# A decode kernel's second MLP weight: 18 rows on each of 96 partitions in place of 13 on 128 and 64 rows apart

## The chip, the core and the metric

The kernel runs on one core of a Trainium2 chip. The core has five engines with instruction streams of their own: TensorE (PE; its weight loads are listed as PEld), VectorE (DVE), ScalarE (ACT), GpSimd (POOL) and SyncE (SP), which here only issues transfers. They meet by semaphores. Sixteen transfer (DMA) engines move data between the chip's main memory and the on-chip memory of 128 partitions; SP and ACT each have a queue that feeds all sixteen. The metric is the device time of one execution in microseconds, lower being better. Before the change it is 1282.53 us, the median of three runs (1282.53 to 1282.58).

## The reference, cut to what matters

One step of decoding for eight sequences. Two branches work on the same normalized input and are added to it: attention over a cache of 4096 keys with 32 heads, and an MLP.

```python
def _A_ref(x, k_cache, v_cache, wq, wo):          # x: 8 x 1 x 640
    q = (x @ wq).reshape(B, Sq, 32, 128).transpose(0, 2, 1, 3)
    scores = einsum("bhqd,bhkd->bhqk", q, k_cache) * (128 ** -0.5)   # k_cache: 8 x 32 x 4096 x 128
    o = einsum("bhqk,bhkd->bhqd", softmax(scores), v_cache)
    return o.transpose(0, 2, 1, 3).reshape(B, Sq, 32 * 128) @ wo

def _B_ref(x, w1, b1, w2, b2):                    # w1: 640 x 1728, w2: 1728 x 640
    h = gelu(layernorm(x) @ w1 + b1)
    return h @ w2 + b2

xn = layernorm(x)
return x + _A_ref(xn, ...) + _B_ref(xn, ...)
```

All inputs are bf16. The two caches are 537 MB together; everything else is under 15 MB.

## The kernel before

The attention is cut into 32 steps (NQ): each takes one sequence and eight heads, so that a tile of K or V holds 256 keys on each of 128 partitions (16 partitions to a head), 64 KB to a partition, 8.4 MB in all. There are three such slots in the on-chip memory (`S_sb`): two for K in turn (KA, KB) and one for V. In each step VectorE multiplies 176 of the 256 keys with the query and adds up; TensorE transposes the other 80 and multiplies them; ScalarE takes the exponentials; TensorE sums V with 256 small matmuls.

The order of work is written by hand. Every piece is put at a position by `at(position, function)` (lines 775 to 863), step i having positions from 100 i on, and the pieces are then run in order of position; each appends its instructions to the stream of its engine and takes the tickets (semaphore values) of what it needs. PE, DVE and ACT replay their streams as hardware loops; that of PE (`_replay_pe`, line 163) has 32 turns, and what belongs to the last steps alone, the MLP with it, stands inside the loop behind branches that skip it in all other turns.

SP issues nearly all transfers, in one queue: A_wq, then K and V of each step. A load of K waits until the K of two steps before has been used by TensorE and VectorE (`load_k`, line 356), a load of V until the V before has been used (`load_v`, line 369). `load_mlp` (line 364) waits for the K of step 30 to be used, whose slot then takes the MLP's weights, and issues w1 and the larger part of w2. V of step 31 is issued next, and then, once the last K has been used, five pieces of A_wo (`load_wl`, `load_wn`).

ACT issues the few small loads: x, b2 and the last 64 rows of w2 (w2b) at the start, b1 near the end, and the store of the result.

The MLP's weights lie as follows. w1 (640 x 1728) has five rows on each of 128 partitions. F = 1728 = 13 x 128 + 64: w2's first 1664 rows are laid 13 to a partition, so partition p has rows 13p to 13p + 12, one run of 16,640 bytes; the last 64 rows have a small tile of their own, one row to a partition. `pe_mlp1` (line 494) works out the hidden layer in 14 chunks: chunk c < 13 takes w1's columns c, c + 13, c + 26, ... (128 of them), so that its results stand on the partitions where w2's rows for them are; the fourteenth takes the last 64 columns. Each chunk is five matmuls over the input and one for the bias, into a region of a bank of the accumulator memory (`HT_ps`, 8 columns to a chunk). `act_gelu` (line 505) applies the gelu in two instructions, one to 128 partitions and 13 chunks, one to 64 partitions and the last. `pe_mlp2` (line 512) multiplies with w2, five matmuls to a chunk, and adds to the bank that holds the final sum.

On TensorE the MLP stands in the last turn between V's matmuls of step 30 and those of step 31 and among the selections (`pe_selw`, `pe_sel`), which bring the attention's outputs into the layout of A_wo and whose results VectorE folds (`dve_foldw`, `dve_fold`). After V's matmuls of step 31 come the products with A_wo (`fin_wl`, `fin_wn`), a transpose and the store.

Of the kernel before, what the change touches and what calls it, by code (L numbers as in the profile page):

```python
# [8 lines left out]
BF = mybir.dt.bfloat16  # L9
F32 = mybir.dt.float32  # L10
I32 = mybir.dt.int32
ACT = mybir.ActivationFunctionType
AX = mybir.AxisListType

P = 128
# [177 lines left out]
def bass_parallel_sum__gqa_block_cached__mixer_channel_mlp__decode_kernel(  # L193
# [13 lines left out]
    B, _, D = A_x.shape  # L207
    _, H, SK, DH = A_k_cache.shape
    F = B_w1.shape[1]
# [4 lines left out]
    NHQ = H // HS  # L214
    NQ = NHQ * B
    DC = D // P
    FB = F // P
    FLAST = F - FB * P
    SCALE = float(DH) ** -0.5
    TPB = 8  # L220
    NS = 2
# [3 lines left out]
    KA, KB, VS = 0, 1, 2  # L225
# [24 lines left out]
    with ExitStack() as es:  # L250
        sb = lambda name, shape, dt: es.enter_context(nc.sbuf_tensor(name, shape, dt))
        ps = lambda name, shape, dt: es.enter_context(nc.psum_tensor(name, shape, dt))
        sem = lambda name: es.enter_context(nc.semaphore(name))
# [4 lines left out]
        def part(slot, lo, n, rows=P):  # L258
            return S_sb[0:rows, slot, lo:lo + n]
# [3 lines left out]
        def scratch(n, rows=P, slot=KB):  # L263
            ap = part(slot, o_[slot], n, rows)
            o_[slot] += n + n % 2
            return ap

        wq_sb = part(VS, 0, DC * H * DH).rearrange("p (c n) -> p c n", c=DC)
        w1_sb = scratch(DC * F, P, KA).rearrange("p (c n) -> p c n", c=DC)
        w2_sb = scratch(FB * D, P, KA).rearrange("p (c n) -> p c n", n=D)  # L270
        hT_sb = scratch((FB + 1) * B, P, KA).rearrange("p (c b) -> p c b", b=B)
        b1_sb = scratch(F, 1, KA)
        selW_sb = scratch(HW * P, P, KA).rearrange("p (c h r) -> p c h r", c=HW, h=HW)
        sel_sb = scratch(HS * P, P, KA).rearrange("p (c h r) -> p c h r", c=HS, h=HS)
# [13 lines left out]
        assert max(o_.values()) <= SLOT  # L288

        ones_sb = sb("ones_sb", [1, B], BF)  # L290
        w2b_sb = sb("w2b_sb", [FLAST, D], BF)
        xT_sb = sb("xT_sb", [P, 2, DC, B], BF)
        KT_sb = sb("KT_sb", [P, NS, TPB, P], BF)
        Sd_sb = sb("Sd_sb", [P, 2, NKEY], F32)
# [26 lines left out]
        TR_ps = ps("TR_ps", [P, 2, TPB * P], BF)  # L321
# [4 lines left out]
        ACC_ps = ps("ACC_ps", [P, 512], F32)  # L326
        TRB, SBK = [_Bank(), _Bank()], [_Bank(), _Bank()]
        PVB, QBB, CHB, ACCB = _Bank(), _Bank(), _Bank(), _Bank()
        QT_ps = CH_ps[:, 0:H * B]
        HT_ps = TR_ps[:, 1, :].bitcast(F32)[:, 0:(FB + 1) * B]  # L330
        RS_ps = CH_ps[:, 384:384 + HS]
        OUT_ps = QB_ps[:, :].bitcast(BF)
        assert H * B <= 384
# [1 line left out]
        pe, dve, act, sp, pool = (_Eng(sem(f"{n}_s")) for n in ("pe", "dve", "act", "sp", "pool"))  # L335
        pe2, act2 = _Eng(sem("pe2_s")), _Eng(sem("act2_s"))
        ld_s = [_Dma(sem(f"ld_s{s}")) for s in range(3)]
        ld_x, ld_b1, ld_b2, ld_wq, ld_w1, ld_w2a, ld_w2b, st_o = (
            _Dma(sem(n)) for n in ("ld_x", "ld_b1", "ld_b2", "ld_wq", "ld_w1", "ld_w2a", "ld_w2b", "st_o"))
        ld_vl = [_Dma(sem(f"ld_vl{q}")) for q in range(1, len(V_CUT) - 1)]  # L340
        ld_wl = [_Dma(sem(f"ld_wl{q}")) for q in range(2)]
        ld_wn = [_Dma(sem(f"ld_wn{q}")) for q in range(len(WN_CUT) - 1)]
        tk = {}
        prog = []

        def at(pos, fn, *a):
            prog.append((pos, len(prog), fn, a))

        def load(key, dma, dst, src, eng=None):
            tk[key] = dma.sig((eng or sp).dma_start(dst, src))  # L350
# [13 lines left out]
        def load_mlp():  # L364
            sp.wait(tk[("kt", NQ - 2)], tk[("km", NQ - 2)])
            load("w1", ld_w1, w1_sb, B_w1.rearrange("(p c) f -> p c f", c=DC))
            load("w2a", ld_w2a, w2_sb, B_w2[0:FB * P, :].rearrange("(p c) n -> p c n", c=FB))

        def load_v(i):
            sp.wait(tk["qmm"] if i == 0 else tk[("pv", i - 1)])  # L370
# [117 lines left out]
                pe.matmul(ACC_ps[:, c * B:(c + 1) * B], b2_sb[:, c * P:(c + 1) * P], ones_sb[:, :],  # L488
                          start=False, stop=False, skip_group_check=True)

        def fcols(c):
            return (slice(c, FB * P, FB), P) if c < FB else (slice(FB * P, F), FLAST)

        def pe_mlp1():
            pe.wait(tk["w1"], tk["b1"], tk[("xT", 1)])
            TRB[1].use(pe)
            for c in range(FB + 1):
                cols, rows = fcols(c)
                o = HT_ps[0:rows, c * B:(c + 1) * B]
                for kc in range(DC):  # L500
                    pe.matmul(o, w1_sb[:, kc, cols], xT_sb[:, 1, kc, :], start=(kc == 0), stop=False)
                last = pe.matmul(o, b1_sb[:, cols], ones_sb[:, :], start=False, stop=True)
            TRB[1].used(pe, pe.sig(last))

        def act_gelu():
            TRB[1].use(act)
            act.activation(hT_sb[:, 0:FB, :].rearrange("p c b -> p (c b)"), HT_ps[:, 0:FB * B],
                           ACT.Gelu_apprx_tanh)
            tk["h"] = TRB[1].used(act, act.sig(act.activation(
                hT_sb[0:FLAST, FB, :], HT_ps[0:FLAST, FB * B:(FB + 1) * B], ACT.Gelu_apprx_tanh)))  # L510

        def pe_mlp2():
            pe.wait(tk["h"], tk["w2a"], tk["w2b"])
            for fc in range(FB + 1):
                rows = P if fc < FB else FLAST
                w = w2_sb[:, fc, :] if fc < FB else w2b_sb
                for c in range(DC):
                    last = pe.matmul(ACC_ps[:, c * B:(c + 1) * B], w[:, c * P:(c + 1) * P],
                                     hT_sb[0:rows, fc, :], start=False, stop=False, skip_group_check=True)
            tk["mlp"] = ACCB.used(pe, pe.sig(last))  # L520


# [254 lines left out]
        at(-898, load, "b2", ld_b2, b2_sb, B_b2.rearrange("(o f) -> o f", o=1), act)  # L777
        at(-890, load, "wq", ld_wq, wq_sb, A_wq.rearrange("(p c) n -> p c n", c=DC))
        at(NQ * Q - 55, load_mlp)
        at(-897, load, "w2b", ld_w2b, w2b_sb[:, :], B_w2[FB * P:F, :], act)  # L780
        at(-870, load_k, 0)
        at(-800, consts_pool)
        at(-795, idents)
# [10 lines left out]
        at(-765, cp_q)  # L794
        at(NQ * Q - 11.8, load_b1)
        at(NQ * Q - 11.5, pe_mlp1)
        at(NQ * Q - 11, act_gelu)
        at(NQ * Q + 4.6, pe_mlp2)
        for i in range(NQ):
            o = i * Q  # L800
            last = i == NQ - 1
# [8 lines left out]
            w = 42.0 / nt  # L810
# [20 lines left out]
        o = NQ * Q  # L831
# [76 lines left out]
```

## Time and profile before

| | |
|---|---|
| median of three runs | 1282.53 us |
| profiled execution | 1282.34 us |
| its span, first to last instruction | 1281.0 us |
| busy: VectorE / TensorE / ScalarE / GpSimd | 1103.0 / 672.2 / 476.1 / 100.0 us |
| moved | 551.99 MB, 431 GB/s over the span |
| TensorE's granted clock, mean | 0.557 |

The span is the time between the first and the last instruction of the execution that was profiled; the rest of its time lies around it. "Busy" is the time in which an engine has at least one instruction under way. The profile has further views: forty equal slices of the span with the busy tenths of each engine and of the transfer engines; the transfers by queue and by issue, with the time from issue to landing; the chain that ended last, followed back from the end; the timeline, in which each row has its start, its duration, engine, line, operation, and in brackets how long the engine had been idle and what ended that; and tables of busy time and GB/s by windows. In them q1 is SP's queue, q10 is ACT's, and q8 and q14 fetch instructions. Nearly all instructions carry line 111, that of the helper which emits them, so they are told apart by the tiles that they write and read; w1, w2 and A_wo lie in `S_sb`, as K and V do. The trace also has a record of every packet: one row of a transfer, moved by one of the sixteen engines, with its queue, start, duration and bytes.

### The profile page before, as it was taken

How to read it: one execution, taken by the hardware profiler on the slowest of the kernel's cores; microseconds unless marked ns; L12 is line 12 of the kernel's file. 1: busy time of each engine (PE TensorE's matmuls, PEld its weight loads, DVE VectorE, ACT ScalarE, POOL GpSimd, SP SyncE). 2: the span in 40 equal slices, each digit the busy share in tenths (PEclk: the TensorE clock that was granted, in tenths of full speed). 3: DMA queues.
4: the chain of work that ended last, by engine and by line, in shares of the span. 5: the costliest groups of instructions: out<-in, count | busy, mean ns of one | idle time of the engine just before them, and what ended most of it. 6: DMA issues, size and time to landing. Idle time of an engine off the chain costs nothing.

```text
span 1281.0 us, 34439 instructions
## 1 busy us (share of the span) xinstructions
PE 672.2 (52%) x13944; PEld 575.5 (45%) x13944; DVE 1103.0 (86%) x680; ACT 476.1 (37%) x905; POOL 100.0 (8%) x110
## 2 busy tenths in 40 slices
PE   1546555446545446555456554456454466464476
PEld 1435445345534345444345444345343355353365
DVE  1899999889888899888898888898888898888895
ACT  0524444233444233443234443234443234442331
POOL 0000010000000000000000000000000000000040
PEclk9755565555555555555565565555555565555565
DMA  9999999999999999999999999999999999999998
GB/s 400 445 422 436 432 432 434 434 436 432 432 432 440 428 432 436 440 426 432 438 438 428 430 436 442 428 430 436 440 430 428 436 436 436 426 438 432 432 439 361
DMA packets 10675, 551.99 MB, mean 431 GB/s; under 512 B 1244, under 2 KB 1445, under 8 KB 1702
## 3 DMA queue, kind: packets, MB, share of 16 engines
q1 hardware_dynamic: 10512, 551.70, 99.7%
q8 instruction: 9, 0.15, 0.0%
q10 hardware_dynamic: 150, 0.11, 0.0%
q14 instruction: 4, 0.03, 0.0%
HBM read 551.80 MB, written 0.01 MB: 431 GB/s over the span
## 4 chain that ended last, share of the span: by engine, by line
DMA 52%; DVE 36%; issue 11%; DVEq 0%; PE 0%; SPq 0%; ACT 0%
DMA S_sb<-in_A_k_cache_dram 51%; DVE S_sb L111 26%; DVE Sd_sb L111 8%; DMA S_sb<-in_A_wo_dram 2%; DVE S_ps L111 1%; DVE ri_sb L111 0%; DVEq L109 0%; PE ACC_ps L111 0%; DVE mx_sb L111 0%; SPq L111 0%; DVE mbT_sb L111 0%; DVE mxT_sb L111 0%; DVE mq_sb L111 0%; DVE mb_sb L111 0%; PE QB_ps L111 0%
## 5 line engine op out<-in xcount | busy, mean ns | idle before, releaser
L111 PE MATMUL TR_ps<-ident_bf,S_sb 128*128 128x128 bf16 (+1 forms) x2570 | 342.9, 280 | 353.5 <-POOL kr_sb L111 341.6
L111 DVE TENSOR_TENSOR S_sb<-S_sb,qbc_sb 128x7552 bf16<-128x7552 bf16 (+1 forms) x96 | 392.6, 4089 | 128.4 <-DMA S_sb<-in_A_k_cache_dram 128.1
L111 PEld LDWEIGHTS TR_ps<-ident_bf,S_sb 128*128 (+2 forms) x2570 | 245.4, 103 | 411.6 <-issue 337.7
L111 DVE TENSOR_REDUCE Sd_sb<-S_sb 128x59 f32<-128x3776 bf16 (+1 forms) x96 | 390.2, 4064 | 6.0
L111 ACT ACTIVATE KT_sb<-TR_ps 128x1024 bf16<-128x1024 bf16 x320 | 326.5, 1023 | 122.0 <-PE TR_ps L111 110.9
L111 PE MATMUL PV_ps<-P_sb,S_sb 128*128 128x8 bf16 x8192 | 224.0, 175 | 137.4 <-DMA S_sb<-in_A_v_cache_dram 134.5
L111 PEld LDWEIGHTS PV_ps<-P_sb,S_sb 128*128 128x128 bf16 x8192 | 221.5, 103 | 140.1 <-DMA S_sb<-in_A_v_cache_dram 137.3
L111 DVE TENSOR_TENSOR S_sb<-S_sb 128x3776 bf16<-128x3776 bf16 (+1 forms) x96 | 204.6, 2131 | 3.3
L111 ACT ACTIVATE P_sb<-Sd_sb,NB_sb 128x256 bf16<-128x256 f32 x256 | 126.3, 494 | 213.4 <-DVE NB_sb L111 213.4
L111 PE MATMUL S_ps<-qrep_sb,KT_sb 128*128 128x8 bf16 x2560 | 121.9, 177 | 51.6 <-ACT KT_sb L111 48.4
L111 ACT ACTIVATE oU_sb<-PV_ps 128x8 f32<-128x8 f32 x31 | 5.5, 177 | 375.6 <-PE PV_ps L111 375.6
L111 PEld LDWEIGHTS S_ps<-qrep_sb,KT_sb 128*128 128x128 bf16 x2560 | 91.8, 103 | 83.0 <-ACT KT_sb L111 42.1
L111 POOL TENSOR_TENSOR oT_sb<-oU_sb,ri_sb 128x8 bf16<-128x8 f32 x31 | 71.8, 2315 | 378.8 <-DVE S_sb L111 303.2
L111 POOL COPY qrep_sb<-qT_sb 128x128 bf16<-128x128 bf16 x32 | 14.5, 453 | 475.3 <-PE S_ps L111 455.2
L111 ACT ACTIVATION_READ_ACCUMULATOR P_sb<-Sd_sb,NB_sb 128x1 f32 x256 | 47.8, 187 | 0.0
L111 DVE TENSOR_TENSOR S_ps<-S_ps,mask_sb 128x320 f32<-128x320 f32 (+1 forms) x65 | 31.6, 486 | 2.6 <-PE S_ps L111 2.6
L111 DVE TENSOR_REDUCE Sd_sb<-S_ps 128x40 f32<-128x320 f32 x64 | 31.5, 491 | 2.2
L111 PE MATMUL QB_ps<-ident_bf,qrep_sb 128*128 128x128 bf16 x32 | 9.1, 284 | 41.2 <-DVE S_sb L111 21.4
L111 ACT ACTIVATE qbc_sb<-QB_ps 128x128 bf16<-128x128 f32 x32 | 8.9, 277 | 58.0 <-PE QB_ps L111 58.0
L111 POOL MEMSET kr_sb<- 128x1 f32 x32 | 3.1, 98 | 294.7 <-DMA S_sb<-in_A_k_cache_dram 294.7
L111 PEld LDWEIGHTS QB_ps<-ident_bf,qrep_sb 128*128 128x128 bf16 x32 | 3.3, 103 | 44.1 <-ACT oU_sb L111 29.5
L111 PE MATMUL CH_ps<-rs_sb,ones_f 128*128 128x8 f32 x64 | 16.5, 330 | 6.6 <-ACT P_sb L111 6.6
(71 smaller groups left out, 147.0 us busy)
## 6 DMA issues: line engine op xcount, KB each, us to landing
S_sb<-in_A_v_cache_dram SPq DMA_DIRECT2D x1, 6144.0 KB, 26.8
S_sb<-in_A_wq_dram SPq DMA_DIRECT2D x1, 5120.0 KB, 16.0
S_sb<-in_A_wo_dram SPq DMA_DIRECT2D x1, 2560.0 KB, 16.5
S_sb<-in_B_w_dram SPq DMA_DIRECT2D x1, 2160.0 KB, 30.3
S_sb<-in_B_w_dram SPq DMA_DIRECT2D x1, 2080.0 KB, 34.8
S_sb<-in_A_v_cache_dram SPq DMA_DIRECT2D x1, 2048.0 KB, 31.3
S_sb<-in_A_wo_dram SPq DMA_DIRECT2D x1, 1280.0 KB, 19.3
S_sb<-in_A_wo_dram SPq DMA_DIRECT2D x1, 800.0 KB, 20.8
```

Source lines behind the costliest of these rows:

```text
L111: inst = getattr(e, name)(*a, **k)
```

## The change

F = 1728 is also 18 x 96. w2 is loaded in one transfer, with 18 rows on each of 96 partitions: partition p has rows 18p to 18p + 17, one run of 23,040 bytes, and partitions 96 to 127 get none of it. The separate tile and its load on ACT's queue are gone. The hidden layer is worked out in 18 chunks of 96 columns (c, c + 18, c + 36, ...), the gelu is one instruction on 96 partitions, and the outer layer has 18 times five matmuls over 96 rows. w1's layout, the positions of the pieces and all other work are as before.

```diff
-    FB = F // P
-    FLAST = F - FB * P
+    FP = 96
+    FB = F // FP
+    assert FB * FP == F
...
-        w2_sb = scratch(FB * D, P, KA).rearrange("p (c n) -> p c n", n=D)
-        hT_sb = scratch((FB + 1) * B, P, KA).rearrange("p (c b) -> p c b", b=B)
+        w2_sb = scratch(FB * D, FP, KA).rearrange("p (c n) -> p c n", n=D)
+        hT_sb = scratch(FB * B, FP, KA).rearrange("p (c b) -> p c b", b=B)
...
-        w2b_sb = sb("w2b_sb", [FLAST, D], BF)
...
-        HT_ps = TR_ps[:, 1, :].bitcast(F32)[:, 0:(FB + 1) * B]
+        HT_ps = TR_ps[:, 1, :].bitcast(F32)[0:FP, 0:FB * B]
...
-            load("w2a", ld_w2a, w2_sb, B_w2[0:FB * P, :].rearrange("(p c) n -> p c n", c=FB))
+            load("w2", ld_w2, w2_sb, B_w2.rearrange("(p c) n -> p c n", c=FB))
...
-        def fcols(c):
-            return (slice(c, FB * P, FB), P) if c < FB else (slice(FB * P, F), FLAST)
-
         def pe_mlp1():
             pe.wait(tk["w1"], tk["b1"], tk[("xT", 1)])
             TRB[1].use(pe)
-            for c in range(FB + 1):
-                cols, rows = fcols(c)
-                o = HT_ps[0:rows, c * B:(c + 1) * B]
+            for c in range(FB):
+                o = HT_ps[:, c * B:(c + 1) * B]
                 for kc in range(DC):
-                    pe.matmul(o, w1_sb[:, kc, cols], xT_sb[:, 1, kc, :], start=(kc == 0), stop=False)
-                last = pe.matmul(o, b1_sb[:, cols], ones_sb[:, :], start=False, stop=True)
+                    pe.matmul(o, w1_sb[:, kc, c:F:FB], xT_sb[:, 1, kc, :], start=(kc == 0), stop=False)
+                last = pe.matmul(o, b1_sb[:, c:F:FB], ones_sb[:, :], start=False, stop=True)
...
-            act.activation(hT_sb[:, 0:FB, :].rearrange("p c b -> p (c b)"), HT_ps[:, 0:FB * B],
-                           ACT.Gelu_apprx_tanh)
             tk["h"] = TRB[1].used(act, act.sig(act.activation(
-                hT_sb[0:FLAST, FB, :], HT_ps[0:FLAST, FB * B:(FB + 1) * B], ACT.Gelu_apprx_tanh)))
+                hT_sb.rearrange("p c b -> p (c b)"), HT_ps, ACT.Gelu_apprx_tanh)))
...
-            pe.wait(tk["h"], tk["w2a"], tk["w2b"])
-            for fc in range(FB + 1):
-                rows = P if fc < FB else FLAST
-                w = w2_sb[:, fc, :] if fc < FB else w2b_sb
+            pe.wait(tk["h"], tk["w2"])
+            for fc in range(FB):
                 for c in range(DC):
-                    last = pe.matmul(ACC_ps[:, c * B:(c + 1) * B], w[:, c * P:(c + 1) * P],
-                                     hT_sb[0:rows, fc, :], start=False, stop=False, skip_group_check=True)
+                    last = pe.matmul(ACC_ps[:, c * B:(c + 1) * B], w2_sb[:, fc, c * P:(c + 1) * P],
+                                     hT_sb[:, fc, :], start=False, stop=False, skip_group_check=True)
...
-        at(-897, load, "w2b", ld_w2b, w2b_sb[:, :], B_w2[FB * P:F, :], act)
```

More of the change, by code (lines that the diff above doesn't have):

```diff
@@ L337, in bass_parallel_sum__gqa_block_cached__mixer_channel_mlp__decode_kernel @@
         ld_s = [_Dma(sem(f"ld_s{s}")) for s in range(3)]
-        ld_x, ld_b1, ld_b2, ld_wq, ld_w1, ld_w2a, ld_w2b, st_o = (
-            _Dma(sem(n)) for n in ("ld_x", "ld_b1", "ld_b2", "ld_wq", "ld_w1", "ld_w2a", "ld_w2b", "st_o"))
+        ld_x, ld_b1, ld_b2, ld_wq, ld_w1, ld_w2, st_o = (
+            _Dma(sem(n)) for n in ("ld_x", "ld_b1", "ld_b2", "ld_wq", "ld_w1", "ld_w2", "st_o"))
         ld_vl = [_Dma(sem(f"ld_vl{q}")) for q in range(1, len(V_CUT) - 1)]
```

## The prediction

> **What bounds the kernel now.** I read the page's slices first, then the table of transfers, the chain that ended last, the last 40 us instruction by instruction, and the traffic by windows.
>
> ```profile
> span 1281.0 us, 34439 instructions
> DMA  9999999999999999999999999999999999999998
> ...
> q1 hardware_dynamic: 10512, 551.70, 99.7%
> q8 instruction: 9, 0.15, 0.0%
> q10 hardware_dynamic: 150, 0.11, 0.0%
> ```
>
> The transfer engines are at nine tenths or more in all slices but the last, and one queue (q1, SP's) has 99.7% of their time. Nothing else needs to be fast; it must only keep that queue filled.
>
> ```profile
> S_sb<-in_B_w_dram SPq DMA_DIRECT2D x1, 2160.0 KB, 30.3
> S_sb<-in_B_w_dram SPq DMA_DIRECT2D x1, 2080.0 KB, 34.8
> ...
> w2b_sb<-in_B_w_dram ACTq DMA_DIRECT2D x1, 80.0 KB, 14.3
> ```
>
> These are w1, w2a and w2b. w2a, issued with w1, lands 4.5 us after it: it stands in line, and 2080 KB at the 434 GB/s of the windows below need 4.9 us. Among the packet records of the trace each of w2a's 128 rows (16,640 B) took 0.62 us, eight in a row on each of 16 engines: 5.0 us. A row of K or V (65,536 B) took 2.42 us; all of these are 27 GB/s to an engine, steady to some ns, and all of them write 128 partitions.
>
> ```profile
> 1205.00 0.81 SPq L111 DMA_DIRECT2D S_sb<-in_A_v_cache_dram  x2
> 1211.57 0.80 SPq L111 DMA_DIRECT2D S_sb<-in_B_w_dram  x2
> 1238.89 0.33 SPq L111 DMA_DIRECT2D S_sb<-in_A_v_cache_dram  x1
> 1255.65 2.23 SPq L111 DMA_DIRECT2D S_sb<-in_A_wo_dram  x5
> ```
>
> This is SP's timeline: the order in which the queue works off V of step 30, w1, w2, V of step 31 and the five pieces of A_wo. By the packet records w2a ends at 1246.3, V at 1265.7, A_wo at 1278.0, with no gap; so each issue has 7 us or more in hand.
>
> ```profile
> 1251.49 4.10 DVE Sd_sb L111
> ...
> 1256.50 20.76 DMA S_sb<-in_A_wo_dram
> 1277.26 0.05 issue
> 1277.30 1.51 PE ACC_ps L111 x40
> ```
>
> The chain in order of time ends in A_wo's landing and 40 matmuls behind it. What delays the slowest of the 16 engines delays the end by the same amount.
>
> ```profile
> 1243.60 0.44 PE L111 MATMUL TR_ps<-xT_sb,S_sb 128*128 128x8 bf16 x5 [4.74 <-issue]
> ...
> 1251.25 0.31 ACT L111 ACTIVATE S_sb<-TR_ps 128x104 bf16<-128x104 f32 x2 [10.67 <-PE TR_ps L111]
> ...
> 1252.85 1.90 PE L111 MATMUL ACC_ps<-S_sb 128*128 128x8 bf16 x65
> ...
> 1258.75 0.58 PE L111 MATMUL QB_ps<-oT_sb,S_sb 128*128 128x56 bf16 x8 [3.24 <-DVE oS_sb L111]
> ...
> 1266.15 6.99 PE L111 MATMUL PV_ps<-P_sb,S_sb 128*128 128x8 bf16 x256 [4.11 <-DMA S_sb<-in_A_v_cache_dram]
> ```
>
> The MLP on TensorE: inner layer from 1243.6, gelu, outer layer; then 3.2 us of waiting for VectorE's fold and 4.1 us for V.
>
> **The change, part by part.**
>
> *Inner layer in 18 chunks.* 14 chunks took 1243.56 to 1251.25, 0.55 us each, clocked at 0.5. Four more of the same six matmuls are 2.2 us; the 96 wide loads are no shorter than 0.34 us for five (the 64 wide chunk's row) against 0.38, so at most 0.7 us comes off 18 chunks. A stride of 18 columns of w1 in place of 13 is in no row: between nothing and, once more, the 0.24 us by which five strided loads of w1 (0.38) exceed five plain ones of w2 (65 in 1.86, so 0.14) it is up to 4 us in 18 chunks; nothing is taken, for w1's loads are strided already. *Outer layer:* 90 matmuls in place of 70, at 1.90 / 65 = 0.029 us: +0.6 us. Together 2.8 us (1.9 to 7). The waiting above covers it: selection matmuls end at 1255.5 and would at 1258.3, and the next need the fold that ends at 1258.6. The first fold needs its matmuls (1253.0, then 1255.2) only at 1257.2. If the cover were 4 us too short, the 4.1 us before V's matmuls are next. Cost 0.
>
> *One gelu in place of two* (0.31 us for both) takes 0.1 us off ScalarE, which then waits 4.4 us for VectorE: 0. The outer layer's wait for w2 instead of w2a and w2b: w2 lands 8 us before use, and even 5 us later it is in time: 0.
>
> *w2b leaves ScalarE's queue.* Its issue (0.53 us) stood ahead of a table load and of the first square root at 4.34, which waits for VectorE and not for the queue: 0. Its 64 rows of 1280 B went four to an engine, 0.055 us each, between wq's rows: 0.22 us off each engine's line. Beside them wq slowed down:
>
> ```profile
> 8.50:12.00 3.50, 0.32 (x10) 0.23 (x9) 0.03 (x1) 0.00 (x0) 0.00 (x0) 1.00 1.02 410
> ...
> 130.00:470.00 340.00, 183.00 (x3770) 156.44 (x3770) 306.51 (x182) 131.95 (x252) 24.02 (x28) 0.53 1.00 434
> ```
>
> (last columns: granted clock, share of the transfer engines, GB/s). 24 of 434 GB/s in 3.5 us are 0.2 us more, if w2b caused it. So -0.2 to -0.4; I take -0.3.
>
> *w2's 96 rows of 23,040 B.* Six to an engine at 27 GB/s are 6 x 0.857 = 5.14 us, against 8 x 0.62 = 4.96: +0.2 us. That is the whole cost if the engine itself sets the pace. But no row shows a large transfer to fewer than 128 partitions. If the pace is that of the ways into the memory, tied to partitions, a quarter of them stays unused here: evenly shared, 2160 KB at three quarters of 434 GB/s take 6.8 us, +1.7. If engines meet in pairs on the same partitions' way for the whole of it, they go at half pace: 10.2 us, +5.1. So 0 to +5.1 on the slowest engine. The nearest row is w2b's, the only load of many rows that spared partitions: 80 KB are worth 0.19 us and cost 0.4, about half pace. It is small and mixed with wq, so weak; but it points to the upper end, and six rows in fixed order don't share evenly, nor can an engine that gets through early help another. I take +4.1. Nothing gives it back: the queue is full to the end, and V and A_wo follow on the same engines.
>
> [...]
>
> *Code.* 44 more matmuls with their loads are 88 more instructions in TensorE's loop, which skips them in all turns but the last. By the packet records eight of q8's nine packets of 16 KB come at 22 to 103 us, up to the loop's second turn, and one at 1277.7, to which one engine gives 1.1 us. Longer code calls that one up to 1.5 us earlier, ahead of some rows of A_wo; on one engine of 16, so 0 to +1.5, and 0 taken.
>
> **Sum.** The profiled execution took 1282.34 us (span 1281.0 and 1.34 around it), 0.19 below the median of the three runs: 1282.34 - 0.3 + 0.2 + 4.1 = 1286.3 us, 0.3% up.
>
> **The rivals.**
>
> No collision (other side: not slower). The engine's own 27 GB/s holds for any partitions. For it: 0.055 us for 1280 B in w2b's rows and in A_wo's last rows (128 partitions) alike, and all packets scale with their bytes. Against it: the 410 GB/s. 1282.34 - 0.3 + 0.2 = 1282.2. It decides if w2's rows take 0.86 us each.
>
> Collisions evenly shared, some engines waiting a little and all making use of the rest: +1.7, 1283.9. For it: rows differ in phase by up to 1.5 us from engine to engine; against it: the order of rows is fixed.
>
> The loop no longer fits in what TensorE keeps of its code. Now two branches in the first turn wait 5.6 and 7.5 us for code and later ones don't (one row: the query broadcast at 98.87 after 13.57 us of "issue"). If every turn waited so, TensorE's slack of about 12 us before K's arrival and 5 before V's would be used up in part: with 13.6 us added and the 5 before V's matmuls as cover, 30 x 8.6 = 260 us. Against it: the loop is some 1,330 instructions now and 1,420 then, 7% more, and both end in the same 16 KB piece if a stall at the 177th V matmul of turn one marks a piece's edge.
>
> Faster by over 0.2%: 2.6 us less would need more than all w2b ever cost, and the order of code packets on the engines to change in our favour (they account for most of the 1.5 us by which the engines' ends differ).
>
> **How the numbers follow.** 0.2% of this time, 2.6 us, is about what a measurement of this kernel can tell from no change. Chances: collisions near half pace 0.52, 1286.3 with its own range 1285.2 to 1290; no collision 0.25; evenly shared 0.17; code reloaded each turn 0.03; faster 0.03. Slower is 0.52 + 0.03 = 0.55, same 0.25 + 0.17 = 0.42, faster 0.03. The range takes in the first three: from 1281.8 (no collision, 0.4 us more of wq's toll gone) to 1290.0 (+5.1, code packet +1.5, a third engine on one way now and then, +1).
>
> **What the profile would show.** Right: in the order of time, V of step 31 lands 2.6 us or more later after w2, the engines' ends lie further apart, and TensorE's wait before V's 256 matmuls lengthens although the MLP before it is longer; mean GB/s in the stretch of w2 well under 434. wq's landing 0.2 to 0.4 us earlier. TensorE's inner layer near 9.9 us, and the fold's wait near 0.5 us. Wrong: w2 lands 5 us after w1 and the tail is as before (no collision), or gaps named "issue" in every turn and hundreds of q8 packets (code). It would also be wrong if the split of 96 rows over the engines is not six each: on twelve engines eight rows each are 6.9 us, +1.9.

## The result, and the profile after

| | before | after |
|---|---|---|
| median of six runs each | 1282.47 us (1282.32 to 1282.58) | 1291.55 us (1290.6 to 1292.82) |
| profiled execution | 1282.34 us | 1290.6 us |
| its span | 1281.0 us | 1289.0 us |

The change makes the kernel slower by 9.1 us: the ratio is 1.0072, with a 95% interval of 1.0061 to 1.0083. Forecast were 1286.3 us in a range of 1281.8 to 1290.0. So the sign was right, more than half of the size was missing, and the result lies 1.6 us outside the range. The profiled execution is the quickest of the six, 8.3 us above that of before.

The page of the changed kernel, its slices of transfer time, its queues, and some transfers with their time from issue to landing (last column):

```profile
span 1289.0 us, 34525 instructions
...
DMA  9999999999999999999999999999999999999997
...
q1 hardware_dynamic: 10480, 551.79, 99.4%
q8 instruction: 9, 0.15, 0.0%
q10 hardware_dynamic: 70, 0.03, 0.0%
...
S_sb<-in_A_wq_dram SPq DMA_DIRECT2D x1, 5120.0 KB, 15.2
S_sb<-in_A_wo_dram SPq DMA_DIRECT2D x1, 2560.0 KB, 21.9
```

q10 has lost w2b's packets, the first weights land 0.8 us sooner (15.2 us against 16.0), and the code is fetched in nine packets as before. The large piece of A_wo takes 21.9 us to land instead of 16.5, so something ahead of it in the queue got slower. The share of q1 is still over 99%, which could be read as "bound by transfers as before". The chain that ended last, in order of time, says otherwise (start, duration, what):

```profile
1210.93 31.38 DMA S_sb<-in_B_w_dram
1242.31 3.74 issue
1246.05 22.63 PE TR_ps L111 x108
...
1268.70 0.29 ACT S_sb L111
...
1269.01 1.28 ACT L111
...
1270.30 4.05 ACT P_sb L111 x16
...
1275.08 6.87 PE PV_ps L111 x256
...
1282.19 2.28 PE ACC_ps L111 x80
```

Before, this chain ended in A_wo's landing. Now no transfer stands in it after w1: it goes through TensorE's inner layer (108 matmuls, 22.63 us), the gelu (0.29), a table load (1.28), ScalarE's sixteen instructions for the exponentials of step 31 (4.05), V's matmuls and the products with A_wo. The timeline shows the inner layer in detail, with the weight loads (PEld) apart, and V's matmuls of step 31:

```profile
1246.02 0.97 PEld L111 LDWEIGHTS TR_ps<-xT_sb,S_sb 128*96 128x96 bf16 x5 [7.86 <-issue]
1246.05 1.03 PE L111 MATMUL TR_ps<-xT_sb,S_sb 128*96 128x8 bf16 x5 [7.79 <-issue]
1247.00 0.25 PEld L111 LDWEIGHTS TR_ps<-ones_sb,S_sb 1*96 1x96 bf16 x1
1247.27 0.97 PEld L111 LDWEIGHTS TR_ps<-xT_sb,S_sb 128*96 128x96 bf16 x5
...
1274.93 7.00 PE L111 MATMUL PV_ps<-P_sb,S_sb 128*128 128x8 bf16 x256
```

Three readings. Five weight loads of 96 columns take 0.97 us, where five of 128 columns took 0.38 before; a chunk takes 1.25 us instead of 0.55, and 18 chunks 22.6 us. The loads of a chunk follow one another without a gap, so they set the pace and the matmuls follow them; the granted clock was 0.50 in both kernels here, so it is not the cause. The inner layer also begins 2.5 us later than before (1246.05 against 1243.60). And V's matmuls have no bracket any more: the wait for V of 4.11 us is gone, though V itself came late. By the packet records V of step 31 ends at 1270.42 us (before 1265.65), 4.5 us before it is used.

Two things thus got worse at once. The time of TensorE's chain can be added up: 2.5 us of late start and 14.9 us of longer inner layer are 17.4. Behind the inner layer the chain goes through ScalarE. This is the start of the exponentials of step 31, in the timeline before:

```profile
1257.26 0.51 ACT L111 ACTIVATE P_sb<-Sd_sb,NB_sb 128x256 bf16<-128x256 f32 x1 [4.40 <-DVE NB_sb L111]
```

And after:

```profile
1270.30 0.51 ACT L111 ACTIVATE P_sb<-Sd_sb,NB_sb 128x256 bf16<-128x256 f32 x1
```

Before, ScalarE had 4.4 us to spare behind the gelu and its table load, in which it waited for VectorE, and TensorE then waited 4.1 us for V. Both waits are gone. Together they took up 8.5 of the 17.4 us, and V's matmuls begin 8.8 us later (1274.93 against 1266.15). At the end 0.8 us come back: before, the last 80 products with A_wo took 3.0 us, with a wait for a piece of A_wo among them, and now they take 2.3. 8.8 - 0.8 = 8.0, the difference of the spans.

The transfers by themselves would have cost some 5 us. By the packet records each of w2's 96 rows took 1.56 us on average (at most 1.70), where 23,040 bytes at the steady pace of the other rows need 0.857; first rows of V beside them took up to 3.8 us instead of 2.42. A_wo's last packet ends at 1282.79, 4.8 us later than before.

### The profile page after: what moved, and what is told of

The parts are those of the page before. It is cut to its first block, busy times and chain, and to the rows that moved or that the text cites. A ratio compares the mean times of both kernels' runs of the same rounds, so it can differ in the third digit from the quotient of the medians.

```text
span 1289.0 us, 34525 instructions
## 1 busy us (share of the span) xinstructions
PE 684.1 (53%) x13988; PEld 586.5 (46%) x13988; DVE 1102.9 (86%) x680; ACT 476.0 (37%) x904; POOL 104.5 (8%) x110
## 4 chain that ended last, share of the span: by engine, by line
DMA 50%; DVE 35%; issue 11%; PE 3%; ACT 0%; DVEq 0%; SPq 0%
DMA S_sb<-in_A_k_cache_dram 47%; DVE S_sb L111 26%; DVE Sd_sb L111 7%; DMA S_sb<-in_B_w_dram 2%; PE TR_ps L111 2%; DVE S_ps L111 1%; PE PV_ps L111 1%; PE ACC_ps L111 0%; ACT P_sb L111 0%; DVEq L109 0%; DVE ri_sb L111 0%; DVE mx_sb L111 0%; ACT L111 0%; DVE mbT_sb L111 0%; DVE mxT_sb L111 0%
## 5 line engine op out<-in xcount | busy, mean ns | idle before, releaser
L111 POOL COPY qrep_sb<-qT_sb 128x128 bf16<-128x128 bf16 x32 | 19.6, 614 | 472.7 <-PE S_ps L111 453.5
L111 PE MATMUL TR_ps<-xT_sb,S_sb 128*96 128x8 bf16 x90 | 19.0, 324 | 7.8 <-issue 7.8
## 6 DMA issues: line engine op xcount, KB each, us to landing
S_sb<-in_A_wq_dram SPq DMA_DIRECT2D x1, 5120.0 KB, 15.2
S_sb<-in_A_wo_dram SPq DMA_DIRECT2D x1, 2560.0 KB, 21.9
```

Of the source, the lines that this page charges most:

```text
L111: inst = getattr(e, name)(*a, **k)
```

## The experiments

Two theories were on the table. The transfers' theory is the prediction's own: w2 on 96 partitions is loaded at about half pace, and the queue behind it is that much later. TensorE's theory is that the inner layer got so long that its cover is gone, whatever the transfers do. Each was run without the other.

**The load alone.** w2 is loaded as 18 rows on 96 partitions, w2b goes, and all matmuls stay as they were.

```diff
-        w2_sb = scratch(FB * D, P, KA).rearrange("p (c n) -> p c n", n=D)
+        w2_sb = scratch(18 * D, P, KA).rearrange("p (c n) -> p c n", n=D)
...
-        w2b_sb = sb("w2b_sb", [FLAST, D], BF)
+        w2b_sb = w2_sb[0:FLAST, FB, :]
...
-            load("w2a", ld_w2a, w2_sb, B_w2[0:FB * P, :].rearrange("(p c) n -> p c n", c=FB))
+            load("w2", ld_w2, w2_sb[0:96, :, :], B_w2.rearrange("(p c) n -> p c n", c=18))
```

> The kernel before with only the changed load: w2 in one transfer of 96 rows of 23,040 bytes, no w2b; all matmuls as before, so they read parts of w2's tile that hold other rows or old keys, and the MLP's part of the output is not the reference's. Theory (two causes, the load being one): w2's rows take about 1.6 us each instead of 0.86, V of step 31 and A_wo come some 4.8 us later, and the inner layer keeps its 7.7 us: span about 1285.8, time about 1287. Rival (all of it comes from TensorE's matmuls, the slow rows being made up for): about 1282.

Measured: 1287.61 us (1286.86 to 1287.85), ratio 1.0041 (1.0027 to 1.0055), against 1282.37 before on the same chip. w2's rows took 1.56 us, A_wo's last packet ended at 1282.47. Its timeline:

```profile
1246.55 0.44 PE L111 MATMUL TR_ps<-xT_sb,S_sb 128*128 128x8 bf16 x5 [8.49 <-issue]
...
1270.57 7.00 PE L111 MATMUL PV_ps<-P_sb,S_sb 128*128 128x8 bf16 x256 [9.30 <-DMA S_sb<-in_A_v_cache_dram]
```

With the old matmuls TensorE waits 9.30 us for V (4.11 before): here the transfers do set the end, and 5.2 us are their price. The inner layer starts late in this kernel too, 1246.55, and nothing comes of it.

**The matmuls alone.** The hidden layer in 18 chunks of 96 columns, over the old loads.

```diff
-        w2_sb = scratch(FB * D, P, KA).rearrange("p (c n) -> p c n", n=D)
+        w2a_sb = scratch(FB * D, P, KA).rearrange("p (c n) -> p c n", n=D)
+        w2_sb = w2a_sb[0:FP, :, :]
...
-            load("w2a", ld_w2a, w2_sb, B_w2[0:FB * P, :].rearrange("(p c) n -> p c n", c=FB))
+            load("w2a", ld_w2a, w2a_sb[:, 0:13, :], B_w2[0:13 * P, :].rearrange("(p c) n -> p c n", c=13))
...
-            for c in range(FB + 1):
+            for c in range(FB):
...
-                    pe.matmul(o, w1_sb[:, kc, cols], xT_sb[:, 1, kc, :], start=(kc == 0), stop=False)
+                    pe.matmul(o, w1_sb[:, kc, c:F:FB], xT_sb[:, 1, kc, :], start=(kc == 0), stop=False)
```

> The kernel with only the changed matmuls: 18 chunks of 96, but w2a and w2b loaded as before (128 partitions of 16,640 bytes, and 64 single rows), so that the outer layer reads parts of the tile that hold other rows or old keys and the MLP's part of the output is not the reference's. Theory (two causes, the matmuls being one): 1.25 us to a chunk, the inner layer 22.6 us long from about 1243.6, V's matmuls of step 31 start about 1272.5, 6 us after V is there: span about 1286.6, time about 1288. Rival (the load alone): the inner layer slow or not, the time stays at 1282.5.

Measured: 1288.26 us (1287.95 to 1288.47), ratio 1.0045 (1.0029 to 1.0062). Its timeline:

```profile
1244.20 1.03 PE L111 MATMUL TR_ps<-xT_sb,S_sb 128*96 128x8 bf16 x5 [5.37 <-issue]
...
1266.75 1.03 PE L111 MATMUL S_ps<-oT_sb,S_sb 128*128 128x128 bf16 x8
...
1273.08 6.98 PE L111 MATMUL PV_ps<-P_sb,S_sb 128*128 128x8 bf16 x256
```

The inner layer runs from 1244.20 to 1266.75, and V, landed long before, is waited for no more. So TensorE alone costs 5.9 us, more than the transfers alone. The two prices, 5.2 and 5.9, add up to 11.1 and not to 9.1: the two chains run beside each other, and only the later one counts. What makes the changed kernel slower than this one is a link between them: its inner layer starts at 1246.05, 1.85 us later than here, and its profiled span is 1.8 us longer. (The medians differ by 3.3; the changed kernel's runs spread over 2.2 us, and its profiled one is the lowest.)

**The same change with loads 128 wide.** The changed kernel, but each weight load takes 128 columns at the same stride of 18. The 32 results too many go to rows of the accumulator that nobody reads.

```diff
-        w1_sb = scratch(DC * F, P, KA).rearrange("p (c n) -> p c n", c=DC)
+        w1f = scratch(DC * F + 32 * FB, P, KA)
+        w1_sb = w1f[:, 0:DC * F].rearrange("p (c n) -> p c n", c=DC)
...
-                    pe.matmul(o, w1_sb[:, kc, c:F:FB], xT_sb[:, 1, kc, :], start=(kc == 0), stop=False)
+                    pe.matmul(o, w1f[:, kc * F + c:kc * F + c + 127 * FB + 1:FB], xT_sb[:, 1, kc, :], start=(kc == 0), stop=False)
```

> The changed kernel with the weight loads of the inner layer 128 wide at the same stride of 18; the 32 further columns run over into what lies behind, their results stand on partitions 96 to 127 and are not used. Theory (the width of 96 made the weight loads slow): 0.55 us to a chunk, the inner layer 9.9 us, V's matmuls of step 31 wait for V again, which comes late for the load alone: time near the 1287.6 of the load alone. Rival (the stride, or 18 chunks as such): 1.25 us to a chunk and 1291 still.

Measured: 1287.7 us (1287.32 to 1288.4), ratio 1.0043 (1.0027 to 1.0058). Its timeline:

```profile
1246.57 0.44 PE L111 MATMUL TR_ps<-xT_sb,S_sb 128*128 128x8 bf16 x5 [8.44 <-issue]
...
1256.57 1.03 PE L111 MATMUL S_ps<-oT_sb,S_sb 128*128 128x128 bf16 x8
...
1271.06 7.00 PE L111 MATMUL PV_ps<-P_sb,S_sb 128*128 128x8 bf16 x256 [8.01 <-DMA S_sb<-in_A_v_cache_dram]
```

Eighteen chunks now take 10.0 us (the prediction had 9.9), the wait for V is back with 8.01 us, and the time is that of the load alone. More columns are loaded in less than half the time, at the same stride. So the width is the cause and the stride of 18 is not.

**Weight loads of many forms.** Twenty-two chunks of five loads and matmuls each were put behind the inner layer of a kernel with the change: 96 columns wide at strides of 1, 2, 4, 8, 9, 13, 15, 16, 17 and 18, then 128 wide at the same strides, then 64 wide at 1 and 18.

```diff
+            for x, (w, st) in enumerate(
+                    [(96, s) for s in (1, 2, 4, 8, 9, 13, 15, 16, 17, 18)]
+                    + [(128, s) for s in (1, 2, 4, 8, 9, 13, 15, 16, 17, 18)] + [(64, 1), (64, 18)]):
+                o = HTW[0:w, (FB + x) * B:(FB + x + 1) * B]
+                for kc in range(DC):
+                    b = min(kc, 3) * F
+                    pe.matmul(o, w1f[:, b:b + (w - 1) * st + 1:st], xT_sb[:, 1, kc, :],
+                              start=(kc == 0), stop=False)
```

> The changed kernel with 22 more chunks of the inner layer behind its 18, into unused columns of the bank, to time weight loads by form: 96 wide at strides 1, 2, 4, 8, 9, 13, 15, 16, 17, 18, then 128 wide at the same strides, then 64 wide at 1 and 18; the time of the whole is longer for it and says nothing. Theory S (the stride): five loads take as long at 96 as at 128 for a stride, about 0.38 us at 13 and about 0.97 at 18, with a step somewhere between 13 and 18. Theory W (the width: 128 is a fast form that 96 is not): all 128 wide ones are at 0.4 or less, and all 96 wide ones near 0.97 or falling to about 0.5 at stride 1.

Its timeline, weight loads only: 96 wide at stride 1, 8 and 18, then 128 wide at 1, 4, 8 and 18, then 64 wide at 1 and 18.

```profile
1522.53 0.47 PEld L111 LDWEIGHTS TR_ps<-xT_sb,S_sb 128*96 128x96 bf16 x5
...
1524.56 0.96 PEld L111 LDWEIGHTS TR_ps<-xT_sb,S_sb 128*96 128x96 bf16 x5
...
1531.92 0.97 PEld L111 LDWEIGHTS TR_ps<-xT_sb,S_sb 128*96 128x96 bf16 x5
...
1533.16 0.21 PEld L111 LDWEIGHTS TR_ps<-xT_sb,S_sb 128*128 128x128 bf16 x5
...
1533.85 0.25 PEld L111 LDWEIGHTS TR_ps<-xT_sb,S_sb 128*128 128x128 bf16 x5
...
1534.23 0.39 PEld L111 LDWEIGHTS TR_ps<-xT_sb,S_sb 128*128 128x128 bf16 x5
...
1537.53 0.39 PEld L111 LDWEIGHTS TR_ps<-xT_sb,S_sb 128*128 128x128 bf16 x5
...
1538.08 0.34 PEld L111 LDWEIGHTS TR_ps<-xT_sb,S_sb 128*64 128x64 bf16 x5
...
1538.59 0.68 PEld L111 LDWEIGHTS TR_ps<-xT_sb,S_sb 128*64 128x64 bf16 x5
```

| five loads, us | stride 1 | 2 | 4 | 8 | 9 | 13 | 15 | 16 | 17 | 18 |
|---|---|---|---|---|---|---|---|---|---|---|
| 96 wide | 0.47 | 0.47 | 0.53 | 0.96 | 0.93 | 0.93 | 0.96 | 0.97 | 0.96 | 0.97 |
| 128 wide | 0.21 | 0.21 | 0.25 | 0.39 | 0.37 | 0.37 | 0.38 | 0.39 | 0.39 | 0.39 |
| 64 wide | 0.34 | | | | | | | | | 0.68 |

Of these three widths 128 columns is the fast one, by a factor of 2.1 to 2.5 against 96 columns at every stride tried, and even 64 columns take longer than 128 (0.34 against 0.21 us at stride 1, 0.68 against 0.39 at 18). From stride 1 to stride 8 the time of 96 and of 128 columns about doubles (0.47 to 0.96, 0.21 to 0.39), and from 8 to 18 it stays within 0.93 to 0.97 and 0.37 to 0.39 us; 64 columns, which ran at 1 and 18 only, take twice as long at 18. What makes 128 columns the fast width, no row shows.

This kernel took 1578.16 us in its one run, some 287 us more than the changed kernel, and the 22 chunks themselves (1522.5 to 1539.3 us) are 17 of that. The rest is the prediction's third rival, which the changed kernel itself had escaped. Two lines of its page, the slices of transfer time and the queue that fetches code:

```profile
DMA  9998788977888988887988888898778898888760
...
q8 instruction: 289, 4.73, 1.4%
```

And one of its waits (engine, tile, what ended the wait, us in total, times, longest):

```profile
PEld QB_ps L111 <- issue: 585.1, 31, 22.7
```

TensorE's loop is 264 instructions longer here than in the changed kernel (132 more matmuls and 132 more loads). q8 fetches 289 packets of code instead of nine, about nine more for each of 31 turns, and at the query broadcast TensorE waits for "issue" in 31 turns, together 585 us (16.0 us in two turns in the changed kernel): 18.9 us a turn.

**b1 first.** In the changed kernel b1, 3456 bytes in one row that come over ScalarE's queue, is issued by SP instead, ahead of w1.

```diff
         sp.wait(tk[("kt", NQ - 2)], tk[("km", NQ - 2)])
+            load("b1", ld_b1, b1_sb, B_b1.rearrange("(o f) -> o f", o=1))
             load("w1", ld_w1, w1_sb, B_w1.rearrange("(p c) f -> p c f", c=DC))
...
-        at(NQ * Q - 11.8, load_b1)
```

> The changed kernel with b1's one row issued on SP's queue ahead of w1 instead of on ACT's 27 us later. Theory (b1, issued after V's matmuls of step 30 and landing among the slow rows of w2, holds the inner layer back to 1246.0, while w1's last row ends at 1241.4): the inner layer starts about 1242, 4 us earlier, and as TensorE's chain sets the end, the time falls to about 1287.5, where V's late landing takes over. Rival (w1 or the bank is what it waits for, or the end is set elsewhere): 1291.

Measured: 1287.66 us (1287.37 to 1287.75), ratio 1.004 (1.0025 to 1.0055), 3.9 us less than the median of the changed kernel. Its timeline:

```profile
1242.81 1.05 PE L111 MATMUL TR_ps<-xT_sb,S_sb 128*96 128x8 bf16 x5 [4.56 <-DMA S_sb<-in_B_w_dram]
...
1271.73 6.98 PE L111 MATMUL PV_ps<-P_sb,S_sb 128*128 128x8 bf16 x256
```

The inner layer now waits for w1 by name and starts 3.2 us sooner; V's matmuls come 3.2 us sooner as well. This is the link between the two chains. In the changed kernel b1's row was moved at 1243.1 to 1243.4 us by the packet records, and the packet of four bytes that follows it on ACT's queue came only at 1245.0 (1243.07 before the change), 1.6 us after its data; the trace has the last update of b1's semaphore at 1245.96 (1243.50 before) and the first weight load of the inner layer at 1246.02 (1243.56). By the packets' times one slow row of w2 (1243.40 to 1245.00) fits between the two packets without a gap, as on one transfer engine; before the change it was one row of 0.62 us. The records don't name the engine. The chain's 3.74 us of "issue" between w1's landing and the first matmul was that wait.

**Ten loads by themselves.** After the store, ten loads with rows of 23,040 bytes, each waiting for the one before, on different sets of partitions. Nothing else runs.

```diff
+            for lo, n in ((0, 128), (0, 96), (32, 96), (0, 64), (32, 64), (64, 64), (0, 112), (0, 32), (0, 128), (0, 96)):
+                sp.wait(t)
+                t = ld_t.sig(sp.dma_start(S_sb[lo:lo + n, KA, 0:18 * D],
+                                          A_wo[0:18 * n, :].rearrange("(p c) n -> p (c n)", c=18)))
```

> The kernel before, and after its store ten loads alone on the queue, each issued when the one before has landed, all of rows of 23,040 bytes from A_wo: to partitions 0-127, 0-95, 32-127, 0-63, 32-95, 64-127, 0-111, 0-31, and 0-127 and 0-95 again. Theory (ways into the memory tied to partitions, 0-63 on one half of them and 64-127 on the other): 128 partitions about 7 us plus the fixed part; 96 about 9.5 plus the fixed part, longer than 128 although a quarter less is moved; 0-63 and 64-127 about 6.8 plus it, and 32-95 nearer 3.4 plus it if rows are shared out over the engines so that both halves are used. Rival (the row length or the place in main memory makes w2 slow): time goes with the bytes, 96 at 5.1 plus the fixed part, and 0-63, 32-95 and 64-127 alike at 3.4 plus it.

Windows from issue to next issue of that kernel (start and end, length, busy times of the five engines, granted clock, share of the transfer engines, GB/s), for partitions 0 to 127, 0 to 95, 32 to 127, 0 to 63, 32 to 95 and 64 to 127:

```profile
1280.99:1290.47 9.48, 0.00 (x0) 0.00 (x0) 0.00 (x0) 0.00 (x0) 0.00 (x0) 0.50 0.81 312
1290.47:1302.37 11.90, 0.00 (x0) 0.00 (x0) 0.00 (x0) 0.00 (x0) 0.00 (x0) 0.50 0.80 186
1302.37:1314.47 12.10, 0.00 (x0) 0.00 (x0) 0.00 (x0) 0.00 (x0) 0.00 (x0) 0.50 0.81 183
1314.47:1324.53 10.06, 0.00 (x0) 0.00 (x0) 0.00 (x0) 0.00 (x0) 0.00 (x0) 0.50 0.67 147
1324.53:1330.92 6.39, 0.00 (x0) 0.00 (x0) 0.00 (x0) 0.00 (x0) 0.00 (x0) 0.50 0.66 231
1330.92:1340.82 9.90, 0.00 (x0) 0.00 (x0) 0.00 (x0) 0.00 (x0) 0.00 (x0) 0.50 0.68 149
```

| partitions | 0–127 | 0–95 | 32–127 | 0–63 | 32–95 | 64–127 | 0–111 | 0–31 |
|---|---|---|---|---|---|---|---|---|
| issue to next issue, us | 9.48 | 11.90 | 12.10 | 10.06 | 6.39 | 9.90 | 11.40 | 5.93 |
| mean of one row, us | 0.95 | 1.59 | 1.63 | 1.69 | 1.05 | 1.68 | 1.35 | 1.55 |

The means of the sets 0–127 and 32–95 are raised by some rows of up to 2.1 us; their median is 0.855, the steady pace, where that of 0–95 is 1.60 and that of 0–63 is 1.80. The repeats of the first two took 9.63 and 11.78 us. Ninety-six rows take longer than 128 of the same length, with a quarter fewer bytes. The load to partitions 32 to 95 and that to 0 to 63 have the same number of rows, the same bytes and the same source, and differ by 6.39 against 10.06 us. So it is not the row's length or the main memory: which partitions are written decides the pace of these loads. The windows agree with the theory's two halves: 0 to 63 take 10.06 us and 64 to 127 9.90, and 32 to 95, half of them from each, 6.39. The ways themselves are in no record and stay an assumption. The 6.8 us that the prediction worked out for 96 rows evenly shared were too low: six rows to an engine at 1.56 us are 9.4. (The packets of w2 follow one another in sixteen chains of six, so the split over the engines was even.)

**The same bytes on 64 partitions, well and badly placed.** Two kernels with the matmuls of before and w2 as 64 rows of 34,560 bytes, four to an engine, in one transfer, on partitions 32 to 95 and on 0 to 63.

```diff
-            load("w2a", ld_w2a, w2_sb, B_w2[0:FB * P, :].rearrange("(p c) n -> p c n", c=FB))
+            load("w2", ld_w2, w2_sb[32:96, :, :], B_w2.rearrange("(p c) n -> p c n", c=27))
```

> As the load alone (matmuls as before, so the MLP's part of the output is not the reference's), but w2 as 64 rows of 34,560 bytes on partitions 32 to 95. Theory (ways tied to partitions; 32 to 95 lie on both halves): full pace, V and A_wo no later than before, time 1281.8 to 1282.6. Rival (fewer partitions are slower, wherever they lie): half pace or worse, 1287 or more.

> The same as the load on partitions 32 to 95 (64 rows of 34,560 bytes, matmuls as before, the MLP's part of the output not the reference's), but on partitions 0 to 63. Theory (0 to 63 lie on one half of the ways): half pace, 5 us on the whole queue, time about 1287. Rival (place on the partitions is nothing): 1282.

Measured: 1281.91 us (1281.79 to 1282.24) on 32 to 95, ratio 0.9996 (0.9986 to 1.0005); 1288.94 us (1288.52 to 1289.36) on 0 to 63, ratio 1.0049 (1.0032 to 1.0066). The second is 1.9 us above what was expected. In the first a row took 1.28 us, which is the steady pace, in the second 2.69, a little less than half of it. The same window of w2's stretch, first for partitions 32 to 95:

```profile
1241.50:1248.00 6.50, 3.77 (x43) 3.57 (x43) 6.43 (x7) 0.00 (x0) 3.21 (x1) 0.50 1.17 506
```

Then for partitions 0 to 63:

```profile
1241.50:1248.00 6.50, 0.00 (x0) 0.00 (x0) 6.43 (x7) 0.00 (x0) 3.22 (x1) 0.50 0.97 197
```

V's matmuls in the timeline of the first:

```profile
1265.62 7.00 PE L111 MATMUL PV_ps<-P_sb,S_sb 128*128 128x8 bf16 x256 [4.28 <-DMA S_sb<-in_A_v_cache_dram]
```

And in that of the second:

```profile
1273.18 7.00 PE L111 MATMUL PV_ps<-P_sb,S_sb 128*128 128x8 bf16 x256 [10.27 <-DMA S_sb<-in_A_v_cache_dram]
```

A packet's bytes are counted where it starts (the transfer engines' share of that row is 1.17), so 506 GB/s is no rate that was held; as a comparison of the two the rows serve. Seven microseconds lie between two placements of one and the same transfer. The good one is the control for the load alone: it too loads w2 at once and has no w2b. Between these two, profiled execution by profiled execution, lie 1286.86 - 1281.79 = 5.1 us, and A_wo's last packets lie 1282.47 - 1277.48 = 5.0 us apart. That is the price of the 96 partitions on the transfers.

**w2b moved, the rest kept.** Two variants of the kernel before, to see what the small load at the start is worth. In one, w2b is issued by SP behind w2a; in the other also, on partitions 32 to 95 of a zeroed tile of 128, so that the fourteenth chunk is 128 wide too and the gelu one instruction.

```diff
+            load("w2b", ld_w2b, w2b_sb[:, :], B_w2[FB * P:F, :])
...
-        at(-897, load, "w2b", ld_w2b, w2b_sb[:, :], B_w2[FB * P:F, :], act)
```

> The kernel before with w2b's 64 rows issued on SP's queue behind w2a instead of on ACT's at the start. Theory (at the start w2b costs more than its bytes: wq lands 0.6 us later on the mean engine; at its new place it costs about twice its bytes' worth, 0.4 us, for it reaches only one half of the ways): 1282.0 to 1282.3, a tenth to a half us under before. Rival (it costs the same wherever it runs): 1282.4, as before.

```diff
-        w2b_sb = sb("w2b_sb", [FLAST, D], BF)
+        w2b_sb = sb("w2b_sb", [P, D], BF)
...
+            sp.wait(tk["w2z"])
+            load("w2b", ld_w2b, w2b_sb[32:96, :], B_w2[FB * P:F, :])
...
+            tk["w2z"] = pool.sig(pool.memset(w2b_sb[:, :], 0.0))
...
-        at(-897, load, "w2b", ld_w2b, w2b_sb[:, :], B_w2[FB * P:F, :], act)
```

> The kernel before with w2b's 64 rows on partitions 32 to 95 of a tile that is zero elsewhere, issued on SP's queue behind w2a; the fourteenth chunk 128 wide, its first 32 and last 32 rows meeting zeros. Theory (what w2b costs beyond its bytes is its place on partitions 0 to 63): 1281.9 to 1282.1, like the 1281.9 of w2 on partitions 32 to 95, and half a us under both kernels. Rival (the 64 short rows cost it, wherever they lie): 1282.5, as with w2b late on 0 to 63.

Measured: 1282.5 us for the first (ratio 1.0001, 0.9992 to 1.001), 1282.23 for the second (0.9999, 0.999 to 1.0008); neither can be told from no change, and both are above the times expected by the theory (1282.0 to 1282.3, 1281.9 to 1282.1). In the first the opening weights land after 15.2 us instead of 16.0, and yet V of step 31 and A_wo end where they did (1265.65 and 1278.02). The packet records show where the gain went. w1 and w2a still end 0.7 and 0.5 us sooner than before; then come w2b's own rows, and sixteen rows of V that start beside them take 2.6 to 2.9 us instead of 2.42. In the second no row of V is slow, and A_wo ends 0.5 us sooner than before, which the medians don't resolve. No version run here beats the kernel before by what a measurement can tell.

## Where the prediction failed, and what of it was right

**w2's 96 rows collide at near half pace: right, and in size a little low.** The term was +4.1 us between 0 and +5.1, an estimate that no row of before shows; no run shows the ways into the memory or the pairs of engines behind its bounds either. What the runs show in their place: the rows took 1.56 us instead of 0.857, and the load's price is 5.0 us at A_wo's last packet, 5.1 between profiled executions. That is close to the upper bound, half pace all the time. The rivals "no collision" and "evenly shared" are out by the ten loads and by the 64 rows. But the row that I leaned on was misread. The 410 GB/s at the start were put down to w2b's rows; with w2b gone wq's rows still take 1.59 us on average instead of 1.63, where the steady pace (65,536 bytes in 2.42 us) gives 1.51, so most of it has another reason. And windows of a few microseconds count packets where they start, so 410 was no rate; the same window reads 515 in the changed kernel. The right conclusion came from a row that didn't carry it.

**The inner layer's time on TensorE: the step that failed.** The prediction said that "the 96 wide loads are no shorter than 0.34 us for five (the 64 wide chunk's row) against 0.38, so at most 0.7 us comes off 18 chunks", and bounded all of TensorE's part by 1.9 to 7 us. It took a bound from below and, from above, only the stride into account; that a narrower load could be slower was not among the cases. It measured +14.9 us for the inner layer, where the prediction had 2.2 for the four further chunks, so the cost that was put at 0 was 5.9 us with the matmuls alone. The cover was misread too: it was looked for on TensorE, 3.2 and 4.1 us, while the delay went through the gelu to the exponentials, with ScalarE's 4.4 us and V's 4.1 to spare. The prediction had these 4.4 us, but used them only for a shorter gelu. Even the 8.5 us did not reach. (The lower end of its "1.9 to 7" adds up to 2.1: 2.2 - 0.7 + 0.6.) A row of before could have warned: the 64 wide chunk's five loads took 0.34 us with half the columns and without a stride, nearly as long as 0.38 for 128 columns at a stride of 13, while 65 plain loads of 128 columns took 1.86 us, 0.14 for five. By the last, 64 columns took more than twice as long as 128. The stride, to which the prediction gave "up to 4 us", costs nothing from 13 to 18 (0.37 and 0.39 in 128 wide loads).

**What waits for what: one wait missing.** The prediction listed w2's wait but not that of the inner layer for b1, whose small row (1243.1 us) and its semaphore (1245.96) come among w2's rows (1238.98 to 1250.83). Slow rows hold it up: +2.5 us at the start of the inner layer, 3.2 against the version that loads it first. Without it the changed kernel takes 1287.66 us, where the transfers are again about as late as TensorE.

**What sets the end.** "Nothing gives it back", the transfers' delay, is right for a kernel whose TensorE has room. Here the two delays lie side by side, 5.2 and 5.9 us alone, and the end goes by TensorE's. So the right sign is in part luck: the cause that was forecast is real, and alone it gives 1287.61, near the 1286.3, but in the changed kernel it is another one that sets the end. The sign "TensorE's wait before V's 256 matmuls lengthens" holds where the load is changed alone (9.30 us) and with wide loads (8.01); in the changed kernel the wait is gone. "V lands 2.6 us or more later" held (4.8); "inner layer near 9.9 us" held only with loads 128 wide (10.0).

**The smaller terms.** w2b out of the start was put at -0.3 us; the well placed load on 64 partitions, without w2b, ends its transfers 0.54 us sooner than before although +0.2 was forecast for fewer and longer rows, so the term is some -0.5 to -0.7, and too small for the medians. The opening weights landed 0.8 us sooner, where 0.2 to 0.4 were forecast. The gelu's saving, 0, and the outer layer's wait for w2, 0, stand: w2's last packet ends at 1250.83, and the outer layer begins at 1270.30. The longer outer layer was put at +0.6; its 90 matmuls took 2.57 us, and the old 70 took 2.12 with the load alone, so it is +0.45. Code: nine packets as before, as forecast; the version with 264 instructions more shows that the rival was real. That its price comes out about right (260 us worked out, some 270 measured) is in part luck: a turn waited 18.9 us and not 13.6, and had more room than the 5 us that were taken for it: 585 us of waiting cost some 270.

What stays open is by what means the partitions set the pace, why nearly all of w2's rows were slow alike (91 of the 96 took 1.44 us or more), and why the changed kernel's runs spread over 2.2 us where those of before spread over 0.3. The profile is of one execution, and no run was aimed at either.

## What to carry to other kernels

A load or a matmul on fewer partitions or columns was not cheaper here by its share (11.90 us for 96 rows alone against 9.48 for 128; 0.97 us for five weight loads of 96 columns against 0.39 for five of 128 at the same stride): before trading 13 x 128 + 64 for 18 x 96, look in the profile for what a narrower instruction of the same kind takes per column, and let the estimate go up by it as well as down. When a kernel is bound by one resource, list how much room each other chain has and take the largest plausible cost against that room, for two chains that slip together show only the later one. And a small load that a large computation waits for is better issued ahead of the large transfers than beside them, as b1 was here: 1287.66 us against 1291.55.

## What the runs showed of the hardware that was not expected

- Weight loads of 96 columns took 2.1 to 2.5 times as long as those of 128, and those of 64 columns longer than those of 128: 0.47, 0.21 and 0.34 us for five at stride 1. Strides of 8 to 18 elements about doubled the time, to 0.93 to 0.97 us for 96 columns and 0.37 to 0.39 for 128 (64 columns: 0.68 at 18). Loading 128 columns and ignoring 32 results took 10.0 us where 96 columns took 22.6.
- 96 rows on partitions 0 to 95 took longer than 128 rows on all partitions (11.90 against 9.48 us from issue to issue), and 64 rows took 6.39 or 10.06 us depending on whether they started at partition 32 or at 0.
- The packet of four bytes behind a small transfer's row came 1.6 us after the data (0.6 us before the change), and the semaphore's update 0.9 us after that (0.4 before); by the packets' times one slow row of another queue's transfer ran between row and packet.
- TensorE's loop had nine packets of code fetched for it in the whole execution; with 264 instructions more it was 289, some nine to each of 31 turns, and these turns waited for "issue", 18.9 us each on average and 22.7 at most.
